# Hash-bucketed attention and a feed-forward layer in one kernel: work issued by an explicit list, weights cast while loading, uniform fallback added on VectorE, scores in two tiles

## The chip, the core and the metric

One core of a Trainium2 chip runs the kernel. It has five engines with in-order instruction queues of their own: TensorE (PE, matmul, with PEld for its weight loads), VectorE (DVE), ScalarE (ACT), GpSimd (POOL) and SyncE (SP, which here only issues DMAs). They meet at semaphores. The metric is device time in microseconds (us) of one launch.

## The reference, cut to what matters

Attention with a bucket mask: a query sees only keys whose six hash bits are the same as its own. Where no key matches, all scores are equal, and the softmax is uniform: the output is then the mean of all values. The result goes through a layer norm and a two-layer feed-forward block with a residual.

```python
q_bits = (einsum('bhsd,dk->bhsk', q, proj) > 0)       # k likewise
mask   = q_bucket[:, :, :, None] == k_bucket[:, :, None, :]
scores = where(mask, scale * q @ k.T, -1e9)
attn   = softmax(scores);  x = (attn @ v) as (B, S, 512)
xn     = (x - mean) / sqrt(var + 1e-6) * g_ln
out    = x + relu(xn @ w_ch1) @ w_ch2
```

B = 4 batches, 8 heads, 768 positions, 64 per head, w_ch1 512x2048, w_ch2 2048x512, all float32 outside.

## The kernel before, in words

A **unit** u (0 to 11) is 256 queries of one batch, three units to a batch. A **step** s (0 to 71, six to a unit) is one unit's 256 queries against 256 of the 768 keys, for one group g of four heads.

Per step: `scores` (L169) makes 24 matmuls into `sc`, a PSUM tile of four banks. Six bits of the hash `G` are multiplied first, and the two halves of q and k (`qb`, `kb`) are added in the same bank, so that a mismatch in the hash lowers the exponent by much. The four heads lie on four strips of 32 rows of the PE array. `exps` (L187) is one ACT instruction over the whole of `sc` to `E`. `av` (L201) makes 16 matmuls of `E` with the values `vaug` (64 columns and a one, which gives the row sum) into `acc`, two banks. At every third step `fall` (L191) first writes a tiny multiple of the sum of all values into `acc` with two matmuls: that is the uniform fallback. After three steps `normalize` (L213) divides on DVE and takes statistics; after six, `center` (L225) subtracts the mean into `xc`, and `flip` (L235) transposes `xc` into `xnT` by DMA.

Per unit then: `ff1` (L241), eight pieces of eight matmuls of 256 columns into one bank, each with a relu into `hb` on DVE (L252); `ff2` (L254), two times four quarters of four matmuls of 512 columns, each half ended by the residual sum `res` on DVE (L265), which `store` (L270) writes out. PSUM is full: four banks `sc`, two `acc`, one each for the tags `f1` and `f2`. So the next `scores` waits for `exps` of the last one, and an `ff1` in bank f1 for the relu of the one ahead.

Batch 0 is brought in by small pieces (`first`, L304): a 256-column piece of q or k is loaded, transposed on DVE in 32x32 blocks (L288), cast, hashed by four matmuls in float32 (`hf`, L301), and turned to bits (L86). Later batches go by whole groups (`load_x`, `turn_piece`, `cast_full`, `hash_mm`), and their bits are moved into `G` by 16 little DMAs a group (`hash_move`, L133).

Weights: `load_w1` (L311) loads w1 as float32 in four DMAs by SP into two buffers; `cast_w1` (L315) multiplies by g and casts, 16 DVE instructions. `load_w2` (L320) lets POOL issue DMAs that cast on the way.

The order of all this is a key per call: `at(key, fn, ...)` puts a call on a list, the list is sorted, and each engine runs its own instructions in that order. Steps have the key s, and the feed-forward pieces of the unit before are spread between them at 8.5 + 0.375 per piece.

Of the kernel before, what the change touches and what calls it, by code (L numbers as in the profile page):

```python
# [12 lines left out]


@with_exitstack
def kernel(
# [15 lines left out]
    nc = tc.nc  # L32
# [12 lines left out]
    EPS_ROW = 2.0 ** -100  # L45

# [3 lines left out]
    def qk_view(t, b, g):  # L50
        return t[b, 4 * g : 4 * g + 4].rearrange("i (tt r) d -> (i tt) (r d)", tt=TT)

    v_view = [v[b].rearrange("h (tt c kj) d -> c tt h (kj d)", tt=TT, c=CC) for b in range(B)]
    out_view = [out[b].rearrange("(tt c u qt) d -> u c tt (qt d)", tt=TT, c=CC, u=3) for b in range(B)]
    w1ap = moe_w_ch1.rearrange("(o p) h -> p o h", p=P)
    w2ap = moe_w_ch2.rearrange("(o p) d -> p o d", p=P)

    pfull = pool.tile([P, 2, P], F32, name="pfull")
    p32 = pool.tile([P, 2, 32], F32, name="p32")
    bias_sb = pool.tile([P, 1], F32, name="bias_sb")  # L60
    mhalf = pool.tile([P, 2], F32, name="mhalf")
    epsm = pool.tile([P, P], BF16, name="epsm")
    warm = pool.tile([P, 512], BF16, name="warm")
    g_sb = pool.tile([P, NDT], F32, name="g_sb")
# [3 lines left out]
    events = []  # L68

    def at(key, fn, *a):  # L70
        events.append((key, len(events), fn, a))

    qb, kb, G, vaug, vsum = {}, {}, {}, {}, {}
    X, T, vnat = {}, {}, {}
    sc, E, acc = {}, {}, {}
    xt, stats, rstd, xc, xnT, hb, f2, res = {}, {}, {}, {}, {}, {}, {}, {}
# [11 lines left out]
    def new_group(b, g):  # L88
        qb[b, g] = pool.tile([P, 2, S], BF16, name=f"qb{b}{g}", tag="qb", bufs=4)
        kb[b, g] = pool.tile([P, 2, S], BF16, name=f"kb{b}{g}", tag="kb", bufs=4)  # L90
        G[b, g] = pool.tile([P, 2, S], BF16, name=f"G{b}{g}", tag="G", bufs=4)

    def cast_q(eng, b, g, src, lo, hi):
        if eng is nc.scalar:
            nc.scalar.activation(qb[b, g][:, :, lo:hi], src, AF.Copy, scale=QS)
        else:
            eng.tensor_scalar(qb[b, g][:, :, lo:hi], src, QS, None, op0=AOP.mult)  # L97

    def load_x(b, g, t):
        X[b, g, t] = pool.tile([P, KJ * CC * D], F32, name=f"X{b}{g}{t}", tag="X", bufs=3)  # L100
        nc.sync.dma_start(out=X[b, g, t], in_=qk_view((q, k)[t], b, g))

    def turn_piece(b, g, t, n):
        if n == 0:
# [386 lines left out]
```

## Time and profile before

| | |
|---|---|
| median of 3 runs (lowest, highest) | 366.58 us (366.09, 366.65) |
| span of the profiled execution | 363.9 us |
| between span and median | 2.7 us |
| mean granted TensorE clock | 0.948 |
| busy: ACT, POOL | 144.7 us (40%), 100.5 us (28%) |
| matmuls, weight loads | 4281, 4344 (of the records in the trace) |

The span runs from the first to the last instruction. Busy times of engines overlap, and a PE shown busy need not be at its peak: matmuls are pipelined, so what a group of them costs is read from the distance between the start of one group and the start of the next.

### The profile page before, as it was taken

How to read it: one execution, taken by the hardware profiler on the slowest of the kernel's cores; microseconds unless marked ns; L12 is line 12 of the kernel's file. 1: busy time of each engine (PE TensorE's matmuls, PEld its weight loads, DVE VectorE, ACT ScalarE, POOL GpSimd, SP SyncE). 2: the span in 40 equal slices, each digit the busy share in tenths (PEclk: the TensorE clock that was granted, in tenths of full speed). 3: DMA queues.
4: the chain of work that ended last, by engine and by line, in shares of the span. 5: the costliest groups of instructions: out<-in, count | busy, mean ns of one | idle time of the engine just before them, and what ended most of it. 6: DMA issues, size and time to landing. Idle time of an engine off the chain costs nothing.

```text
span 363.9 us, 9678 instructions
## 1 busy us (share of the span) xinstructions
PE 312.7 (86%) x4281; PEld 209.8 (58%) x4344; DVE 183.3 (50%) x373; ACT 144.7 (40%) x76; POOL 100.5 (28%) x106
## 2 busy tenths in 40 slices
PE   8674457989988989989989989898889899897993
PEld 3353335766665666756656657666656567565561
DVE  1427245385662363578444534955624545446341
ACT  2344204662453554445246445533535455442000
POOL 1656142019940010069710010399200100101000
PEclk9989555899999999999999999999999999999899
DMA  7799931991021039860030279700210302203022
GB/s 170 174 243 212 306 112 29 273 260 23 9 64 34 3 88 278 193 141 7 12 78 13 59 204 242 192 7 8 64 35 2 88 2 59 31 2 78 10 59 58
DMA packets 34873, 35.68 MB, mean 98 GB/s; under 512 B 17424, under 2 KB 29712, under 8 KB 34832
## 3 DMA queue, kind: packets, MB, share of 16 engines
q1 hardware_dynamic: 31872, 32.96, 36.0%
q0 software_dynamic: 2112, 2.10, 3.6%
q8 instruction: 34, 0.56, 0.6%
q10 hardware_dynamic: 848, 0.01, 0.2%
q14 instruction: 7, 0.06, 0.1%
HBM read 27.27 MB, written 6.29 MB: 92 GB/s over the span
## 4 chain that ended last, share of the span: by engine, by line
PE 66%; DVE 15%; SPq 5%; DMA 4%; issue 3%; ACT 3%; POOL 1%; ACTq 0%; DVEq 0%; POOLq 0%
PE f L248 19%; PE f L258 18%; PE sc L182 11%; PE acc L206 8%; PE hf L301 4%; SPq L133 4%; DVE hb L252 3%; ACT E L189 3%; PE hp L123 2%; DVE xc L231 2%; DMA w1f<-in_moe_w_ch_dram 2%; DMA xnT<-xc 2%; PE warm L354 2%; DVE x L221 2%; DVE st L223 1%
## 5 line engine op out<-in xcount | busy, mean ns | idle before, releaser
L189 ACT ACTIVATE E<-sc,bias_sb 128x2048 bf16<-128x2048 f32 x72 | 141.6, 1967 | 173.9 <-PE sc L182 173.9
L248 PE MATMUL f<-xnT,w_sb 128*128 128x256 bf16 x768 | 99.7, 274 | 16.3 <-DVE hb L252 13.8
L248 PEld LDWEIGHTS <-w_sb 128*128 128x128 bf16 x768 | 72.4, 98 | 39.1 <-issue 23.0
L252 DVE TENSOR_SCALAR hb<-f 128x512 bf16<-128x512 f32 x96 | 65.6, 683 | 52.7 <-PE f L248 51.4
L258 PE MATMUL f<-w_sb,hb 128*128 128x512 bf16 x321 | 86.9, 385 | 3.5
L232 POOL TENSOR_SCALAR rs<-mv 128x2 f32<-128x2 f32 x12 | 6.1, 512 | 199.6 <-DVE mv L230 199.6
L182 PE MATMUL sc<-qb,kb 32*128 32x256 bf16 x1152 | 54.2, 275 | 0.0
L258 PEld LDWEIGHTS <-hb 128*128 128x128 bf16 x384 | 35.2, 99 | 30.5 <-issue 3.2
L206 PEld LDWEIGHTS <-E 128*128 128x128 bf16 x1152 | 43.1, 100 | 11.4 <-issue 10.5
L206 PE MATMUL acc<-vaug,E 128*128 128x65 bf16 x1152 | 49.5, 198 | 0.0
L265 DVE SCALAR_TENSOR_TENSOR res<-f,rs,x 128x512 f32<-128x512 f32 x24 | 18.0, 751 | 54.7 <-PE f L258 50.7
L182 PE MATMUL sc<-G 6*128 6x256 bf16 x576 | 41.9, 280 | 4.0 <-ACT E L189 3.9
L97 POOL TENSOR_SCALAR qb<-T 128x1536 bf16<-128x1536 f32 (+1 forms) x10 | 30.6, 3059 | 13.4 <-DVE T L288 13.4
L182 PEld LDWEIGHTS <-G 6*128 6x128 bf16 x576 | 15.4, 92 | 29.7 <-issue 28.6
L182 PEld LDWEIGHTS <-kb 32*128 32x128 bf16 x1152 | 30.8, 96 | 2.0
L301 PE MATMUL hf<-T,pfull 128*128 128x256 f32 x48 | 18.1, 514 | 13.6 <-DVE T L288 13.5
L83 DVE STREAM_TRANSPOSE T<-X 128x384 f32<-128x384 f32 x48 | 25.4, 555 | 0.0
L301 PEld LDWEIGHTS hf<-T,pfull 128*128 128x128 f32 x48 | 10.7, 246 | 18.7 <-DVE T L288 17.2
L223 DVE BATCH_NORM_STATS2 st<-x 128x6 f32<-128x256 f32 x48 | 18.1, 418 | 0.8
L221 DVE TENSOR_TENSOR x<-acc,rc 128x512 f32<-128x512 f32 x24 | 16.6, 692 | 0.8
L86 DVE TENSOR_SCALAR G<-hf 128x256 bf16<-128x256 f32 x12 | 5.1, 425 | 23.5 <-PE hf L301 23.5
L219 DVE RECIPROCAL rc<-acc 128x8 f32<-128x8 f32 x24 | 4.9, 205 | 21.1 <-PE acc L206 21.1
(35 smaller groups left out, 147.9 us busy)
## 6 DMA issues: line engine op xcount, KB each, us to landing
vnat<-in_v_dram SPq DMA_DIRECT2D x32, 192.0 KB
out_dram<-res SPq DMA_DIRECT2D x48, 128.0 KB
X<-in_q_dram SPq DMA_DIRECT2D x6, 768.0 KB
X<-in_k_dram SPq DMA_DIRECT2D x6, 768.0 KB
w1f<-in_moe_w_ch_dram SPq DMA_DIRECT2D x4, 1024.0 KB
w_sb<-in_moe_w_ch_dram POOLq DMA_DIRECT2D x4, 512.0 KB, 8.5
X<-in_q_dram SPq DMA_DIRECT2D x6, 256.0 KB
X<-in_k_dram SPq DMA_DIRECT2D x6, 256.0 KB
```

The costliest lines, as they stand in the source:

```text
L83: nc.vector.transpose(d[:, j, kj0 : kj0 + n], s[:, j, kj0 : kj0 + n])
L97: eng.tensor_scalar(qb[b, g][:, :, lo:hi], src, QS, None, op0=AOP.mult)
L182: nc.tensor.matmul(sc[s][:, i, 256 * kk : 256 * kk + 256], lh, rh, start=(rep == 0), stop=(rep == 2), skip_group_check=True,)
L189: nc.scalar.activation(E[s], sc[s], AF.Exp, scale=EXP_SCALE, bias=bias_sb)
L206: nc.tensor.matmul(acc[u, g][:, qt, (D + 1) * i : (D + 1) * (i + 1)], E[s][:, i, 256 * kk + P * qt : 256 * kk + P * qt + P], vaug[u // 3][ ...
L221: nc.vector.tensor_tensor(xo, a[:, :, :, 0:D], rc.to_broadcast([P, 2, 4, D]), op=AOP.mult)
L223: nc.vector.bn_stats(stats[u][:, qt, g], xt[u][:, qt, 256 * g : 256 * g + 256])
L248: nc.tensor.matmul(f1[:, n].rearrange("p (t x) -> p t x", t=2), w1_sb[:, dt, P * nt : P * nt + P], xnT[u][:, :, dt], start=(dt == 0), stop ...
L252: nc.vector.tensor_scalar_max(hb[u][:, 2 * p : 2 * p + 2], f1, 0.0)
L258: nc.tensor.matmul(f2[u, t], hb[u][:, nt, P * t : P * t + P], w2_sb[:, nt], start=(nt == 0), stop=(nt == NNT - 1),)
L265: nc.vector.scalar_tensor_tensor(res[u][:, t], f2[u, t], rstd[u][:, t : t + 1], xt[u][:, t], op0=AOP.mult, op1=AOP.add,)
L301: nc.tensor.matmul(hp[:, :256], pfull[:, j], tp[:, j], start=(j == 0), stop=(j == 1))
```

## The change

The kernel is the same in its arithmetic, apart from where the fallback, g and the casts are done. It has six parts.

- **Order.** The keys are replaced by a list of 1138 words, `ORDER`, each with an operation, the engine that runs it, and its indices: `S.t.14.2` is the scores of step 14 for all heads on TensorE, `R.a.2.4` the relu of unit 2, piece 4, on ACT. Each engine runs its words in the order of the list. Steps are taken out of order within a batch (14, 13, 12, 16), and ff1 pieces of a unit too.
- **Scores.** `sc` becomes two tiles of two banks (two heads each), and `exps` two ACT instructions of half the size, 144 for 72. In steps 0 to 9 the scores and the value matmuls of the two halves are also apart.
- **Fallback.** The 48 matmuls of `fall` go. The sum of the values over all keys is made once for each group of heads and batch by one matmul with ones (`sp`, 8 in all) and copied to `vsB` (`sc`), and a DVE instruction of 520 elements (`na`, 24 in all) adds it to `acc` into an SBUF tile `y`, on which the division works.
- **Weights.** w1 is loaded like w2, by four DMAs of POOL that cast. The 16 casts on DVE go, and g is applied in `ce`, where the centring becomes a DVE instruction with a second tensor (`gB`). The two xnT tiles of unit 0 are transposed by PE (`ft`) and copied (`fc`).
- **Relu.** 43 of the 96 run on ACT, 53 on DVE.
- **Start and end.** 32 warm-up matmuls of 128 columns for 24 of 512; one DMA of proj and copies for four DMAs; stores of the last unit in halves.

```diff
-        sc[s] = psum.tile([P, 4, 512], F32, name=f"sc{s}", tag="sc")
+        return ps(f"sc{s}{h}", [P, 2, 512], ("scA", "scB")[h])
-        nc.scalar.activation(E[s], sc[s], AF.Exp, scale=EXP_SCALE, bias=bias_sb)
+        nc.scalar.activation(E(s)[:, heads(h)], sc(s, h), AF.Exp, scale=EXP_SCALE, bias=bias_sb)
-        for qt in range(2):
-            nc.tensor.matmul(
-                acc[u, g][:, qt, : 4 * (D + 1)], epsm,
-                vsum[u // 3][:, 4 * g : 4 * g + 4].rearrange("p h e -> p (h e)"),
-                start=True, stop=False, skip_group_check=True,
-            )
+        vs = vsB(u // 3)[:, 4 * g : 4 * g + 4].rearrange("p h e -> p (h e)").unsqueeze(1).to_broadcast([P, 2, A])
+        nc.vector.scalar_tensor_tensor(
+            yt(u, g), vs, EPS_ROW, made[f"acc{u}{g}"][:, :, :A], op0=AOP.mult, op1=AOP.add,
+        )
-            nc.vector.tensor_scalar(xc[u][:, qt], xt[u][:, qt], mv[:, qt, 0:1], None, op0=AOP.subtract)
+        nc.vector.scalar_tensor_tensor(
+            xc(u)[:, t], xt(u)[:, t], mv(u)[:, t, 0:1], gB, op0=AOP.subtract, op1=AOP.mult,
+        )
-        nc.sync.dma_start(out=w1f[n], in_=w1ap[:, :, 512 * n : 512 * n + 512])
+        nc.gpsimd.dma_start(out=w1_sb[:, :, 512 * n : 512 * n + 512], in_=w1ap[:, :, 512 * n : 512 * n + 512])
-        nc.vector.tensor_scalar(
-            w1_sb[:, dt, 512 * n : 512 * n + 512], w1f[n][:, dt], g_sb[:, dt : dt + 1], None, op0=AOP.mult,
-        )
+        if eng is nc.scalar:
+            nc.scalar.activation(hb(u)[:, 2 * p : 2 * p + 2], f1, AF.Relu)
+        else:
+            eng.tensor_scalar_max(hb(u)[:, 2 * p : 2 * p + 2], f1, 0.0)
-        for _, _, fn, a in sorted(events, key=lambda e: (e[0], e[1])):
-            fn(*a)
+        for word in ORDER.split():
+            name, eng, *args = word.split(".")
+            OPS[name](ENGINES[eng], *map(int, args))
```

What this moves, at three places. First DVE ahead of the first feed-forward piece. In the kernel before, the casts of w1 (`w_sb`) stand between the last pieces of batch 0 (T and G), each with a weight DMA to wait for:

```order
L316 TENSOR_SCALAR w_sb<-w1f_172,g_sb 128x512 x4
L288 STREAM_TRANSPOSE T_449<-X_201 128x256 x2
L86 TENSOR_SCALAR G_104<-hf_453 128x256
L316 TENSOR_SCALAR w_sb<-w1f_205,g_sb 128x512 x4
L316 TENSOR_SCALAR w_sb<-w1f_460,g_sb 128x512
L288 STREAM_TRANSPOSE T_509<-X_203 128x256 x2
L86 TENSOR_SCALAR G_107<-hf_513 128x256
```

On the same engine of the changed kernel, the statistics and centring of unit 0 (st, mv, xc) stand there, with four transposes of batch 1 (`T_733`, which waits for the DMA of `X_731`) ahead of them:

```order
L442 TENSOR_TENSOR x_424<-y_578,rc_580 128x2x256 [waits DVE_49]
L244 STREAM_TRANSPOSE T_733<-X_731 128x384 [waits DMAHW0_49]
L244 STREAM_TRANSPOSE T_733<-X_731 128x384 x3
L446 BN_STATS st_533<-x_424 128x6 [waits DVE_49]
L446 BN_STATS st_533<-x_424 128x6
L449 BN_AGGR mv_740<-st_533 128x2 [waits DVE_49]
L450 SCALAR_TENSOR_TENSOR xc_742<-x_424,mv_740,gB 128x512 [waits DMAHW2_49,DVE_49]
```

The casts are gone from DVE; a load of the next batch is now ahead of unit 0's centring. Second, POOL in the same part of the program. Before, the four casting DMAs of w2 lie between its casts of kb and sums of values:

```order
L321 DMA w_sb<-in_moe_w_ch_dram 128x4x512
L295 CAST kb_106<-T_274 128x2x256
L321 DMA w_sb<-in_moe_w_ch_dram 128x4x512
L295 CAST kb_106<-T_326 128x2x256
L151 CAST vaug_92<-vnat_91 128x24x64
L321 DMA w_sb<-in_moe_w_ch_dram 128x4x512
```

After it, one DMA of w1 (L315), then the values of group 1 with the waits for their loads, then the three others and w2 (L318):

```order
L315 DMA w_sb<-in_moe_w_ch_dram 128x4x512
L328 CAST vaug_159<-vn_250 128x12x64 [waits DMAHW5_49,DMAHW6_49,DMAHW1_49,DMAHW0_49]
L328 CAST vaug_159<-vn_250 128x12x64
L336 TENSOR_TENSOR t_571<-vn_250 128x768 [waits Pool_49]
L338 TENSOR_TENSOR vsum_325<-t_571 128x256 [waits Pool_49]
L315 DMA w_sb<-in_moe_w_ch_dram 128x4x512 x3
L318 DMA w_sb<-in_moe_w_ch_dram 128x4x512 x3
```

So eight weight DMAs for four stand on POOL, three quarters of w1 behind the last values of batch 0. Third, ACT in the middle of the program. Before, it runs exponentials alone:

```order
L189 ACTIVATE E_2482<-sc_2457,bias_sb 128x2048
L189 ACTIVATE E_2564<-sc_2539,bias_sb 128x2048
L189 ACTIVATE E_2649<-sc_2614,bias_sb 128x2048
L189 ACTIVATE E_2731<-sc_2706,bias_sb 128x2048
L189 ACTIVATE E_2818<-sc_2793,bias_sb 128x2048
```

After it, pairs of halves, with a relu (hb) or a copy of the value sums (vsB) between some:

```order
L411 ACTIVATE E_2426<-sc_2400,bias_sb 128x1024
L411 ACTIVATE E_2426<-sc_2403,bias_sb 128x1024
L485 ACTIVATE hb_2170<-f_37_2434 128x512
L411 ACTIVATE E_2478<-sc_2455,bias_sb 128x1024
L411 ACTIVATE E_2478<-sc_2452,bias_sb 128x1024
...
L411 ACTIVATE E_2723<-sc_2700,bias_sb 128x1024
L351 COPY vsB_1677<-vp_2746 128x4x64
```

A relu on ACT so comes behind a pair of exponentials that may still run, and the next pair behind the relu.

More of the change, by code (lines that the diff above doesn't have):

```diff
@@ L66, with sb @@
     w2_sb = pool.tile([P, NNT, DM], BF16, name="w2_sb")
[L68 to L76, printed above, removed]
+    made = {}
+    def sb(name, shape, dt, tag, bufs):
+        if name not in made:
+            made[name] = pool.tile(shape, dt, name=name, tag=tag, bufs=bufs)
+        return made[name]
@@ L93, in cast_q, with cast @@
[L93 removed]
+    def cast(eng, t, dst, src):
         if eng is nc.scalar:
[L95 to L107 removed]
@@ L235, in flip @@
[L235 to L244 removed]
+            nc.vector.bn_stats(stats(u)[:, qt, g], xt(u)[:, qt, 256 * g : 256 * g + 256])
```

580 lines of the change are left out of this document (309 added, 271 removed).

## Prediction

> **What bounds the kernel now.** I read the page's busy times first, then the busy time by stage, then the timeline of PE in the two stages that differ, and last what PE waited for.
>
> ```profile
> span 363.9 us, 9678 instructions
> PE 312.7 (86%) x4281; PEld 209.8 (58%) x4344; DVE 183.3 (50%) x373; ACT 144.7 (40%) x76; POOL 100.5 (28%) x106
> ```
>
> PE is the only engine near its span. The median of the runs, 366.58 us, is 2.7 us above this span; I make the sum against the span and add 2.7 at the end. Busy by stage (start and end, length, busy time of PE, PEld, DVE, ACT and POOL, then the granted clock, the DMA share, GB/s):
>
> ```profile
> 0.00:10.00 10.00, 7.97 (x28) 3.47 (x28) 1.81 (x6) 1.91 (x2) 1.27 (x11) 1.00 0.82 174
> 10.00:20.00 10.00, 5.98 (x73) 4.13 (x74) 4.14 (x12) 5.07 (x4) 7.19 (x9) 0.95 0.79 174
> 20.00:30.00 10.00, 7.25 (x102) 5.02 (x99) 3.88 (x11) 3.80 (x2) 4.01 (x5) 0.88 1.13 248
> 30.00:40.00 10.00, 6.19 (x74) 3.96 (x74) 7.26 (x15) 2.10 (x2) 6.20 (x6) 0.80 1.08 227
> 40.00:50.00 10.00, 3.15 (x24) 2.08 (x20) 2.93 (x8) 1.97 (x1) 1.49 (x1) 0.50 0.87 282
> 50.00:65.00 15.00, 11.70 (x130) 7.99 (x131) 7.24 (x20) 4.62 (x3) 4.59 (x4) 0.50 0.13 26
> 65.00:337.00 272.00, 249.23 (x3745) 171.20 (x3804) 147.54 (x294) 125.21 (x64) 75.73 (x70) 1.00 0.35 85
> 337.00:341.00 4.00, 4.00 (x17) 1.77 (x15) 0.48 (x1) 0.00 (x0) 0.00 (x0) 0.65 0.01 2
> 358.40:363.90 5.50, 0.00 (x0) 0.00 (x0) 0.73 (x1) 0.00 (x0) 0.00 (x0) 0.98 0.36 95
> ```
>
> There are two kernels here. Up to 65 us PE is thinly used, at a falling clock; from 65 to 358.4 it is busy; then come 5.5 us of residual sum and stores. The timeline shows why the front is long:
>
> ```profile
> 39.06 1.67 DVE L316 TENSOR_SCALAR w_sb<-w1f,g_sb 128x512 bf16<-128x512 f32 x4
> 45.96 0.48 DVE L316 TENSOR_SCALAR w_sb<-w1f,g_sb 128x512 bf16<-128x512 f32 x1 [5.23 <-DMA w1f<-in_moe_w_ch_dram]
> 46.85 2.08 PE L301 MATMUL hf<-T,pfull 128*128 128x256 f32 x4 [5.78 <-DVE T L288]
> 65.00 1.89 PE L248 MATMUL f<-xnT,w_sb 128*128 128x256 bf16 x8
> ```
>
> DVE, in order, stands before a cast for 5.23 us until a w1 DMA lands; the transpose behind it is late, PE idles 5.78 us, the clock drops, and the first piece of ff1 starts at 65.0. By the order of the program 9 steps of scores and 8 of values are done there.
>
> In the dense stage I take the cost of a piece from start to start of groups:
>
> ```profile
> 206.21 0.66 PE L206 MATMUL acc<-vaug,E 128*128 128x65 bf16 x16
> 206.71 1.04 PE L248 MATMUL f<-xnT,w_sb 128*128 128x256 bf16 x8
> 207.58 1.03 PE L258 MATMUL f<-w_sb,hb 128*128 128x512 bf16 x3
> 211.42 0.39 PE L195 MATMUL acc<-vsum,epsm 128*128 128x260 bf16 x2
> 211.65 0.65 PE L206 MATMUL acc<-vaug,E 128*128 128x65 bf16 x16
> 213.96 0.29 PE L182 MATMUL sc<-G 6*128 6x256 bf16 x4
> 214.73 0.66 PE L206 MATMUL acc<-vaug,E 128*128 128x65 bf16 x16
> 352.14 6.21 PE L258 MATMUL f<-w_sb,hb 128*128 128x512 bf16 x27
> 84.83 1.51 PE L123 MATMUL hp<-T,p 128*32 128x192 f32 x32
> ```
>
> Values 0.50 us (206.21 to 206.71), ff1 0.87, fallback pair 0.23, scores 0.77; a quarter of ff2 0.86 (6.21 less some 0.17 of tail, by seven: the program has 28 there, one record is missing); a hash of a group 1.5. From 65.0 the kernel before still has 63 x 0.77 + 64 x 0.50 + 96 x 0.87 + 96 x 0.86 + 21 x 0.23 + 6 x 1.5 = 48.5 + 32 + 83.5 + 82.6 + 4.8 + 9 = 260.4 us of PE work, and takes 293.4. The 33.0 us between are 22.8 of idle (272.0 - 249.2), 1.4 of low clock (4.0 x 0.35), and 8.8 of seams between groups. PE's waits in that stage:
>
> ```profile
> PE f L248 <- DVE hb L252: 13.8, 11, 2.1
> PE hp L123 <- DVE hb L252: 2.4, 3, 0.8
> PE f L248 <- DMA xnT<-xc: 2.3, 2, 1.3
> ```
>
> (In all, how often, the longest.) Mostly ff1 waits for a relu that DVE reaches late.
>
> **The change, part by part.**
>
> *The front.* What must be done before the first ff1 (F.0.5) changes. By the list PE then has 10 hash pieces, 20 half scores, one full, 9 steps of values and the warm-up behind it. A hash piece is 1.04 us at full clock (the 2.08 above is at 0.50). A half of the scores lies between 0.39 (half the work) and 0.77 (two heads share the array where four did, and as many columns stream); I take 0.7, nearer to the full row, since columns set the pace. Sum: 10.4 + 14 + 0.8 + 4.5 and some 3.4 of warm-up = 33 us; from 1.7 us on, 35. ACT needs the exponentials of ten steps:
>
> ```profile
> L189 ACT ACTIVATE E<-sc,bias_sb 128x2048 bf16<-128x2048 f32 x72 | 141.6, 1967 | 173.9 <-PE sc L182 173.9
> L95 ACT ACTIVATE qb<-T 128x512 bf16<-128x512 f32 x2 | 1.2, 624 | 0.0
> L252 DVE TENSOR_SCALAR hb<-f 128x512 bf16<-128x512 f32 x96 | 65.6, 683 | 52.7 <-PE f L248 51.4
> L265 DVE SCALAR_TENSOR_TENSOR res<-f,rs,x 128x512 f32<-128x512 f32 x24 | 18.0, 751 | 54.7 <-PE f L258 50.7 <-DMA X<-in_q_dram 4.0
> L231 DVE TENSOR_SCALAR xc<-x,mv 128x512 bf16<-128x512 f32 x24 | 11.7, 487 | 1.0
> ```
>
> A half (1024 elements) lies between 0.98 us (half of 1967) and 1.25 (two of 624); on the line through 512 and 2048 elements it is 1.07, which I take. 20 x 1.07 = 21.4 us, from about 10 us (an estimate: two of the hash pieces and a transpose come first): 32. The DMAs: on DVE, four transposes of batch 1 stand ahead of unit 0's centring, so F.0.5 waits for X of batch 1.
>
> ```profile
> vnat<-in_v_dram SPq DMA_DIRECT2D x32, 192.0 KB
> w_sb<-in_moe_w_ch_dram POOLq DMA_DIRECT2D x4, 512.0 KB, 8.5
> ```
>
> SP issues 12 pieces of X of 256 KB (128 x 512 floats), 10 loads of values of 192, gB of 256 and that X of 768, 6016 KB; POOL beside it one to three weight DMAs, counted at 512 KB as in the row, or at 1024, as they read float32. By the GB/s of the stages 5960 KB have passed at 30 us and 8230 at 40: 6528 KB at 33, 9088 at 43. Behind this come the transposes, statistics, centring, PE transposes and copies, some 5 us (ten DVE or ACT pieces like those quoted): 38 to 48. PE's own 35 is the lowest end. I take **43**, the middle of the DMAs', since the other engines sum to less. The casts that go (16) are worth this shift, no term of their own.
>
> *What is left for PE at 43 us.* 61 x 0.77 + 63 x 0.50 + 83.5 + 82.6 + 9 + two hash pieces 2.1 + six `sp` matmuls 0.7 = 256.4 us. The fallback's removal is in it (4.8 from 260.4, and 0.7 back).
>
> *The stalls.* The loop scores, exponential, scores is tightest:
>
> ```profile
> 66.89 0.80 PE sc L182 x24
> 67.78 1.98 ACT E L189
> 69.79 0.84 PE sc L182 x24
> ```
>
> 2.90 us from start to start with nothing else between; with two halves (2 x 1.07 for 1.97) 3.07. By the list, PE work between the full scores of two steps sums to 3.0 to 6.1 us; eight places are under 3.07, by 0.56 once (18 to 20) and 0.06 elsewhere: 1.0 us. A relu on ACT (512 elements, 0.62) adds to the loop where it stands behind the pair with under 3.7 us of PE work: at most 20 places of half a microsecond, 10 us. Against it, the 13.8 and 2.4 us of waits for DVE go where relus are on ACT, for there DVE is in `na`, `nb`, `ce`. Idle then is 1 to 20 us; I take 7, as the work between two ff1 pieces mostly exceeds their relu too. With the seams, 8.8, that is **16**. If the cover is gone, the 33.0 of before stay.
>
> *DVE and the rest.* `na` adds 24 x 0.75 (as L265), `ce` 24 x (0.75 - 0.49); 43 relus leave (29 us), the casts leave. DVE ends near 50% again, beside PE, and I cost it at nothing. That cover breaks only if one chain of DVE comes late for the next ff1. The DMA transposes stay on SP between the same small moves: 0 to 2.3 us, in the 7. Start and end: the stores of the last unit in halves, 0 to -1 us of 5.5; I keep 5.5.
>
> A row on two engines of one memory:
>
> ```profile
> 31.72 1.81 POOL L164 TENSOR_TENSOR t<-vnat 128x768 f32<-128x768 f32 x1
> 32.31 3.89 DVE L316 TENSOR_SCALAR w_sb<-w1f,g_sb 128x512 bf16<-128x512 f32 x4
> ```
>
> The four casts took 3.89 us beside POOL's sums and 1.67 without (39.06, above). The Trainium skill, "SBUF — State Buffer", section "Who interferes with whom", says that a DVE instruction with two SBUF inputs, or in a two-port mode, and a GpSimd instruction that reads SBUF exclude each other; the trace agrees as far as the two-port kind goes. The rule speaks against the change: `nb` and `ce` now read two SBUF tensors, 48 instructions that did not. By it, each would stand behind POOL in 28% of cases (POOL's share), for about 1 us: 13 us of DVE, an estimate, and by the row's excess at most 2.2 us a time, 30 us. Either is in DVE's slack, so the sum stays by both.
>
> **Sum.** 43 + 256.4 + 16 + 5.5 = 320.9 us of span, with 2.7 around it **323.6 us**.
>
> **The rivals.**
>
> *A slow front: the clock stays at half.* Before, the clock was 0.50 from 40 to 65 us although PE was busy 11.70 of 15. If the new front has one gap like that of 5.78 us, its 33 us of work take up to twice as long: F.0.5 at 60, the time 60 + 256.4 + 16 + 8.2 = 340.6. For it: many in-order waits on two dozen DMAs. Against it: no weight stands ahead of batch 0's transposes now, and at 7.25 of 10 busy the clock was 0.88. The Trainium skill, "TensorE: Matmul & The Clock Gate", section "What's actually happening", says that an idle window of about 3.4 us halves the clock and a busy one restores it. The drop agrees; the return does not, in the 15 us quoted. By the rule the price would be smaller, one window. Chance 0.14.
>
> *The dense stage does not tighten.* The places may be chosen with other durations than the chip's; then other waits take the place of the 13.8, and 33.0 stay: 43 + 256.4 + 33.0 + 5.5 + 2.7 = 340.6. For it: the exponential's loop has 0.7 us of slack on average (3.8 of work against 3.07). Against it: that slack is everywhere positive or nearly so. Chance 0.14.
>
> *Slower: relus queue behind exponentials.* ACT is in order. If each of the 43 relus there waits for a whole pair (2.14 us), then runs 0.62, and PE has but one ff2 quarter (0.86) to cover it, PE loses 1.9 us each: 323.6 + 82 = 405. It passes 366.6 from 1.0 us each on. Against it: the list puts two to four groups behind most such relus. Chance 0.06.
>
> *It does not do what it says.* The first ff1 stays at 65 because the eight casting DMAs come late, and the stalls stay: 65 + 256.4 + 33.0 + 8.2 = 362.6. For it: three quarters of w1 are issued behind the last values of batch 0. Chance 0.04.
>
> **How the numbers follow.** The forecast has 0.62; with F.0.5 from 36 to 48 and 2 to 20 of idle its own range is 312 to 341. The first two rivals end inside 342, so the range is 310 to 342 and leaves out the last two and a little below, under 0.2. Faster by over 0.2% (about what a measurement here can tell from no change): 0.62 + 0.14 + 0.14 + most of 0.04 = 0.93; same 0.01; slower 0.06.
>
> **What would show it.** First ff1 in the timeline at 36 to 48 us, and the clock near 1.00 in 20 to 40. No L195 group; half exponentials of 0.98 to 1.25 us. From the first ff1 to the last matmul 272 us; PE idle there about 7, with no wait for a relu of over 1 us on average. Wrong it would be if `f` waits for ACT, if a POOL weight DMA is what ff1 or ff2 waits for, or if the front's clock is 0.50.

## The result, and the profile after

| | before | after |
|---|---|---|
| median (lowest, highest) | 366.63 us (366.09, 368.04), 5 runs | 321.83 us (319.59, 326.67), 5 runs |
| ratio, 95% interval | 1 | 0.8766 [0.8730, 0.8802] |
| span of the profiled execution | 363.9 us | 325.0 us (its time 326.67 us) |
| first ff1 matmul (F.0.5) | 65.0 us | 51.65 us |
| from there to the last matmul | 293.4 us | 268.3 us |

The profiled execution is the longest of the five, with a granted clock (the share of its full speed that TensorE is given) of 0.957 where the other four (319.59 to 322.12 us) had 0.980 to 0.983, so its front is longer than that of a usual run; ratios, here and below, leave out runs over 1.5% above the fastest of their kernel. The head of the page of after, and its row of the granted clock in 40 slices:

```profile
span 325.0 us, 9793 instructions
PE 310.7 (96%) x4320; PEld 211.8 (65%) x4320; DVE 182.9 (56%) x356; ACT 182.0 (56%) x198; POOL 91.5 (28%) x102
PEclk9995558999999999999999999999999999999999
```

PE is shown busy nearly as long as before (310.7 us for 312.7) in a span 39 us shorter. Busy time by stage, cut at the drop of the clock, at F.0.5 and behind the last matmul (start and end, length, busy time of PE, PEld, DVE, ACT and POOL, then the granted clock, the DMA share, GB/s):

```profile
0.00:24.00 24.00, 17.47 (x200) 13.21 (x201) 11.66 (x36) 11.02 (x11) 7.81 (x20) 1.00 0.99 211
24.00:51.65 27.65, 27.38 (x293) 18.23 (x291) 16.65 (x37) 13.74 (x13) 13.92 (x18) 0.51 1.05 202
51.65:320.00 268.35, 265.81 (x3834) 180.40 (x3830) 153.79 (x283) 157.20 (x174) 69.74 (x64) 1.00 0.33 84
320.00:325.00 5.00, 0.00 (x0) 0.00 (x0) 0.75 (x1) 0.00 (x0) 0.00 (x0) 0.96 0.22 52
```

The dense stage (third row) has 268.35 - 265.81 = 2.5 us of idle for 22.8 before. The front is now 24 us at the full clock, in which PE is busy for 17.47, and 27 us at half of it, in which PE is busy without a break. The run of the median has a span of 320.1 us; if its dense stage and end are as long as here, its first ff1 is at 320.1 - 268.3 - 5.0 = 46.8 us (an estimate). Of the 44.8 us between the medians the dense stage then gives 25.0 and the front 18. What PE waited for in the whole span (in all, how often, the longest):

```profile
PE hf L306 <- DVE tp L244: 4.2, 4, 2.4
PE vp L343 <- POOL vsum L338: 1.4, 2, 0.8
PE f L477 <- DVE hb L487: 0.5, 1, 0.5
PE sc L405 <- ACT E L411: 0.2, 1, 0.2
```

The waits for a relu (13.8 and 2.4 us before) have come down to 0.5, that for `xnT` (2.3) is gone, and no wait on an exponential of more than 0.2 us came in. The groups of the page that answer to those shown of before (busy, mean ns of one, idle time ahead and what ended it):

```profile
L411 ACT ACTIVATE E<-sc,bias_sb 128x1024 bf16<-128x1024 f32 x144 | 153.7, 1111 | 82.2 <-PE sc L405 80.3
L487 DVE TENSOR_SCALAR hb<-f 128x512 bf16<-128x512 f32 x53 | 36.6, 691 | 63.8 <-PE f L477 63.5
L485 ACT ACTIVATE hb<-f 128x512 bf16<-128x512 f32 x43 | 25.6, 596 | 20.6 <-PE f L477 20.5
L433 DVE SCALAR_TENSOR_TENSOR y<-vsB,acc 128x520 f32<-128x520 f32 x24 | 16.5, 689 | 9.0 <-PE acc L420 8.7
L450 DVE SCALAR_TENSOR_TENSOR xc<-x,mv,gB 128x512 bf16<-128x512 f32 x24 | 19.9, 829 | 0.9
```

ACT and DVE wait for PE (80.3, 63.5, 20.5 us), not PE for them. Last, three chains of the front. PE (some of its rows; start, length, and in brackets the idle time and what ended it):

```profile
23.18 1.13 PE L306 MATMUL hf<-tp,pfull 128*128 128x256 f32 x4 [2.42 <-DVE tp L244]
38.45 0.40 PE L343 MATMUL vp<-vsum,ones 128*128 128x256 bf16 x1
47.96 1.50 PE L420 MATMUL acc<-vaug,E 128*128 128x65 bf16 x24
49.27 1.04 PE L464 MATMUL ft<-ident,xc 128*128 128x128 bf16 x8
51.65 2.86 PE L477 MATMUL f<-xnT,w_sb 128*128 128x256 bf16 x24
```

DVE in the same stretch:

```profile
38.89 0.42 DVE L353 COPY vsB<-vp 128x256 f32<-128x256 f32 x1 [4.48 <-PE vp L343]
40.93 1.95 DVE L244 STREAM_TRANSPOSE T<-X 128x384 f32<-128x384 f32 x4
44.69 0.75 DVE L450 SCALAR_TENSOR_TENSOR xc<-x,mv,gB 128x512 bf16<-128x512 f32 x1
```

And POOL:

```profile
29.16 1.79 POOL L328 CAST vaug<-vn 128x768 bf16<-128x768 f32 x2 [3.31 <-DMA vn<-in_v_dram]
34.09 0.73 POOL L338 TENSOR_TENSOR vsum<-t 128x256 bf16<-128x256 f32 x1
```

POOL waits for the last load of the values and has their sums at 34.8. `vp` needs the sums, but stands in PE's queue behind scores and values at half clock, and runs at 38.45. DVE sat idle 4.48 us for it; the four transposes behind it, which need X of batch 1, waited for nothing. The centring is done at 45.4; PE takes the transposes of `xc` at 49.27, busy until then.

### The profile page after: what moved, and what is told of

Its sections match the earlier page's. It is cut to its first block, busy times and chain, and to the rows that moved or that the text cites. A ratio compares the mean times of both kernels' runs of the same rounds, so it can differ in the third digit from the quotient of the medians.

```text
span 325.0 us, 9793 instructions
## 1 busy us (share of the span) xinstructions
PE 310.7 (96%) x4320; PEld 211.8 (65%) x4320; DVE 182.9 (56%) x356; ACT 182.0 (56%) x198; POOL 91.5 (28%) x102
## 4 chain that ended last, share of the span: by engine, by line
PE 78%; DMA 8%; DVE 6%; SPq 4%; POOL 2%; issue 1%; ACT 0%; DVEq 0%; ACTq 0%
PE f L477 24%; PE f L492 23%; PE sc L405 17%; PE acc L420 11%; DMA X<-in_q_dram 4%; DMA vn<-in_v_dram 3%; SPq L382 2%; PE hp L370 2%; DVE xc L450 2%; DMA X<-in_k_dram 2%; PE hf L306 2%; SPq L292 1%; DVE st L446 1%; DVE x L442 1%; DVE y L433 1%
## 5 line engine op out<-in xcount | busy, mean ns | idle before, releaser
L411 ACT ACTIVATE E<-sc,bias_sb 128x1024 bf16<-128x1024 f32 x144 | 153.7, 1111 | 82.2 <-PE sc L405 80.3
L487 DVE TENSOR_SCALAR hb<-f 128x512 bf16<-128x512 f32 x53 | 36.6, 691 | 63.8 <-PE f L477 63.5
L405 PE MATMUL sc<-qb,kb 32*128 32x256 bf16 x1152 | 62.9, 281 | 0.0
L405 PEld LDWEIGHTS <-kb 32*128 32x128 bf16 x1152 | 35.5, 98 | 3.2
L485 ACT ACTIVATE hb<-f 128x512 bf16<-128x512 f32 x43 | 25.6, 596 | 20.6 <-PE f L477 20.5
L336 POOL TENSOR_TENSOR t<-vn 128x768 f32<-128x768 f32 x8 | 15.2, 1905 | 34.6 <-DMA vn<-in_v_dram 20.2
L328 POOL CAST vaug<-vn 128x768 bf16<-128x768 f32 x16 | 13.9, 889 | 39.0 <-DMA vn<-in_v_dram 30.3
L433 DVE SCALAR_TENSOR_TENSOR y<-vsB,acc 128x520 f32<-128x520 f32 x24 | 16.5, 689 | 9.0 <-PE acc L420 8.7
L450 DVE SCALAR_TENSOR_TENSOR xc<-x,mv,gB 128x512 bf16<-128x512 f32 x24 | 19.9, 829 | 0.9
L306 PE MATMUL hf<-tp,pfull 128*128 128x256 f32 x48 | 15.1, 447 | 5.2 <-DVE tp L244 4.2
L442 DVE TENSOR_TENSOR x<-y,rc 128x512 f32<-128x512 f32 x24 | 18.4, 767 | 0.8
```

The costliest lines, as they stand in the source:

```text
L306: nc.tensor.matmul(hf(g, t, kp)[:, :256], pfull[:, j], tp(g, t, kp)[:, j], start=(j == 0), stop=(j == 1))
L405: nc.tensor.matmul(sc(s, i // 2)[:, i % 2, 256 * kk : 256 * kk + 256], lh, rh, start=(rep == 0), stop=(rep == 2), skip_group_check=True,)
L411: nc.scalar.activation(E(s)[:, heads(h)], sc(s, h), AF.Exp, scale=EXP_SCALE, bias=bias_sb)
L433: nc.vector.scalar_tensor_tensor(yt(u, g), vs, EPS_ROW, made[f"acc{u}{g}"][:, :, :A], op0=AOP.mult, op1=AOP.add,)
L442: nc.vector.tensor_tensor(xo, a[:, :, :, 0:D], rc.to_broadcast([P, 2, 4, D]), op=AOP.mult)
L450: nc.vector.scalar_tensor_tensor(xc(u)[:, t], xt(u)[:, t], mv(u)[:, t, 0:1], gB, op0=AOP.subtract, op1=AOP.mult,)
```

## The experiments

"Dense" is the stretch from F.0.5 to the end of the last matmul in the profiled execution. A ratio is to the kernel before on the same chip.

**Is it the order of the list, or the parts?**

*e3: all relus on DVE, the list otherwise the same.*

```diff
-R.v.0.4 R.a.0.3 S.t.10.2 E.a.10.0 F.t.0.2 R.a.0.2 tu.v.1.0.1.2 CA.p.1.0.1 na.v.1.0 A.t.9.0 A.t.11.2 nb.v.1.0
+R.v.0.4 R.v.0.3 S.t.10.2 E.a.10.0 F.t.0.2 R.v.0.2 tu.v.1.0.1.2 CA.p.1.0.1 na.v.1.0 A.t.9.0 A.t.11.2 nb.v.1.0
...
```

> The changed kernel with all 96 relus on DVE (43 moved back from ACT), the list otherwise the same. Theory A (the split of the relus is what took away the 13.8 us of waits for DVE): DVE 183 + 43 x 0.69 - 0 = 213 us busy, PE waits for hb of 8 to 20 us come back, time 328 to 342. Rival (the order alone did it): waits for hb under 3 us, time within 3 us of 321.8.

Measured: 361.88 us (361.07 to 362.72), ratio 0.9893 [0.9841, 0.9945], more than any theory allowed. F.0.5 was at 48.74, so the front is not where it went; dense rose to 307.1 us. PE's waits:

```profile
PE f L477 <- DVE hb L487: 15.3, 10, 4.4
PE f L492 <- DVE res L497: 8.8, 5, 3.8
PE acc L420 <- DVE y L433: 5.0, 5, 1.8
PE hp L370 <- DVE hb L487: 3.0, 1, 3.0
```

DVE was busy 208 of 361 us, far from full, and yet the waits came back and spread to the residual sum and to `na`. (The last row is the hash of a later batch.) The relus do not add up to a full engine; 43 of them now stand in DVE's queue at places where `na`, `nb`, statistics and centring of a unit run, and each thing behind comes late. The waits cost more than their own time: in the dense stage the clock was at half in four stretches, 17.1 us in all, where after has none; that is 8.5 us of the 38.8 by which the stage is longer.

*e7: the kernel before, every other relu on ACT, in the old order.*

```diff
-        nc.vector.tensor_scalar_max(hb[u][:, 2 * p : 2 * p + 2], f1, 0.0)
+        if p % 2:
+            nc.scalar.activation(hb[u][:, 2 * p : 2 * p + 2], f1, AF.Relu)
+        else:
+            nc.vector.tensor_scalar_max(hb[u][:, 2 * p : 2 * p + 2], f1, 0.0)
```

> The kernel before with one part alone: the relus of odd ff1 pieces on ACT, 48 of 96, nothing else moved. Theory A (the waits for hb are DVE's load): of 13.8 us half or more go, time 355 to 361. Theory B (a place in the order is worth more than the engine: relus now stand behind exponentials of 1.97 us): waits of ff1 for ACT of 10 us or more come instead, time 364 to 380.

Measured: 365.81 us (364.77 to 367.48), ratio 1.0025 [1.0002, 1.0048]. One row of PE's waits says why nothing came of it:

```profile
PE f L248 <- DVE hb L255: 13.7, 11, 1.9
```

13.7 us for 13.8: taking half of the relus off DVE left the waits as they were. In the old order the late relus are those behind a unit's normalisation and centring, and that they share an engine with the other 48 did not matter: nine of the eleven waits are of 1.17 us in both kernels, each for the relu that stands behind the second `xc` of a unit. No ff1 waited for ACT either, so the waits bear out neither theory.

*e6: the kernel before, w1 by casting DMAs, and g in the centring, in the old order.*

```diff
-        nc.sync.dma_start(out=w1f[n], in_=w1ap[:, :, 512 * n : 512 * n + 512])
+        nc.gpsimd.dma_start(out=w1_sb[:, :, 512 * n : 512 * n + 512], in_=w1ap[:, :, 512 * n : 512 * n + 512])
-            nc.vector.tensor_scalar(xc[u][:, qt], xt[u][:, qt], mv[:, qt, 0:1], None, op0=AOP.subtract)
+            nc.vector.scalar_tensor_tensor(
+                xc[u][:, qt], xt[u][:, qt], mv[:, qt, 0:1], gB, op0=AOP.subtract, op1=AOP.mult,
+            )
```

> The kernel before with one part of the change alone: w1 by four casting DMAs of POOL at the same keys, no casts on DVE, g applied in the centring. Theory A (the weights' casts on DVE held the front): DVE's wait of 5.23 us and PE's idle of 5.78 us go, first ff1 at 50 to 58 us instead of 65.0, time 350 to 359. Theory B (the old keys hold the front whatever the casts do): first ff1 at 62 to 66, time 363 to 369.

Measured: 368.01 us (363.50 to 372.65, 10 runs), ratio 1.0017 [0.9970, 1.0064]. F.0.5 came at 61.34, 3.7 us earlier, and the dense stage gave it back:

```profile
PE f L250 <- DVE hb L254: 19.7, 11, 2.6
PE hf L303 <- DVE T L290: 9.9, 6, 4.3
```

The waits for a relu grew from 13.8 to 19.7: the centring, now 0.75 us instead of 0.49, stands ahead of it twice, and the nine waits of 1.17 us became 1.71. These 5.9 us are most of the 9.4 by which the dense stage is longer (302.8 us); the rest goes with the half clock, in three stretches of 3.41 us where before had one. The place of F.0.5 lies between the two theories; the time is as the second had it.

*e10: the kernel before with both of these and the fallback on DVE, in the old order, scores in one tile.* The edits of e6 and e7, and

```diff
+        vp = psum.tile([P, 512], F32, name=f"vp{b}{hs}", tag="f1")
+        nc.tensor.matmul(
+            vp[:, : 4 * (D + 1)], epsm, vsum[b][:, hs : hs + 4].rearrange("p h e -> p (h e)"), start=True, stop=True,
+        )
+        nc.vector.tensor_copy(vsB[b][:, hs : hs + 4].rearrange("p h e -> p (h e)"), vp[:, : 4 * (D + 1)])
-        for qt in range(2):
-            nc.tensor.matmul(
-                acc[u, g][:, qt, : 4 * (D + 1)], epsm,
...
+        nc.vector.scalar_tensor_tensor(
+            y, vs, EPS_ROW, acc[u, g][:, :, : 4 * (D + 1)], op0=AOP.mult, op1=AOP.add,
+        )
```

> The kernel before with three parts of the change together, in the old order and with the scores in one tile of four banks: the weights of the first feed-forward layer by casting DMAs with g in the centring, every other relu on ScalarE, and the uniform fallback by the sum of the values on VectorE. Theory A (the new order makes the gain; the parts only move load): 360 to 370 us. Theory B (the parts make it once they are together, since then no engine is in the way): under 345 us.

Measured: 399.04 us (397.12 to 400.02), ratio 1.0927 [1.0879, 1.0976]: worse than either theory. PE's waits:

```profile
PE f L257 <- DVE hb L264: 28.7, 13, 3.2
PE vp L171 <- POOL vsum L167: 18.8, 8, 6.1
PE hf L313 <- DVE T L300: 7.2, 6, 2.9
```

With `na` and the dearer centring on DVE the waits for a relu doubled, and PE stood 18.8 us before the eight sums. That second wait is owed to where I put the sum, behind POOL's addition of the values; in the list it costs 1.4 us. Both are matters of place. F.0.5 was at 60.2 us, so the loss is in the dense stage, 329.7 us: PE is idle there for 43.0 us (22.9 before), and its clock is at half in ten stretches of 3.41 us (one before). So these parts without the list cost 34 us, a good part of it by where the sums were put, the list without the relus on ACT loses 40 of its 45, and together they give all of it. The list with the other parts as before was not run, so how much the order gives alone stays open.

**Two score tiles.**

*e8: after, with one tile of four banks, and from step 10 on one exponential of 2048 elements.*

```diff
-        return ps(f"sc{s}{h}", [P, 2, 512], ("scA", "scB")[h])
+        return ps("scall", [P, 4, 512], "sc")[:, 2 * h : 2 * h + 2]
-        nc.scalar.activation(E(s)[:, heads(h)], sc(s, h), AF.Exp, scale=EXP_SCALE, bias=bias_sb)
+        if s < 10:
+            nc.scalar.activation(E(s)[:, heads(h)], sc(s, h), AF.Exp, scale=EXP_SCALE, bias=bias_sb)
...
+            nc.scalar.activation(E(s), ps("scall", [P, 4, 512], "sc"), AF.Exp, scale=EXP_SCALE, bias=bias_sb)
```

> The changed kernel with scores in one tile of four banks and one exponential of 2048 elements a step from step 10 on (62 of 72 steps; the list is the same, the exponential stands at the place of the second half). Theory A (halves buy nothing by themselves, they cost ACT 0.25 us a step): ACT 182 - 62 x 0.25 = 166 us busy, time within 2 us of 321.8. Theory B (the first half frees two banks early, and the values of a step or the next scores start sooner for it): PE waits for the exponential come up, time 325 to 335.

Measured: 340.40 us (340.17 to 341.18), ratio 0.9330 [0.9305, 0.9354]: outside both theories. Busy times of its front and of its dense stage but for the last 0.5 us, and PE's longest wait, all of it ahead of F.0.5:

```profile
28.00:65.00 37.00, 29.00 (x273) 19.00 (x275) 15.67 (x33) 14.17 (x14) 12.17 (x16) 0.50 0.86 155
65.70:334.00 268.30, 261.88 (x3789) 180.47 (x3830) 151.67 (x283) 147.52 (x112) 69.25 (x64) 1.00 0.31 81
PE scall L406 <- ACT E L413: 11.3, 11, 1.3
```

Dense is 268.8, for 268.3 in after. What is lost is in the front (F.0.5 at 65.7 us), where the halves of a step are apart in the list and the one tile makes each wait for the other's exponential; there the clock was at 0.50 for 37.5 us too. So the two tiles earn their keep in the first ten steps only.

**The fallback.**

*e4: 48 matmuls of zeros of the size of `fall` put back at their old place, ahead of the values.*

```diff
+        if first:
+            for qt in range(2):
+                nc.tensor.matmul(acc[:, qt, :A], ones, zz, start=True, stop=False, skip_group_check=True)
-                        start=(first and kk == 0 and i == range(4)[heads(h)][0]),
+                        start=False,
```

> The changed kernel with 48 matmuls of 260 columns put back on PE, two ahead of each group's values, here with zeros as the moving operand (the fallback stays on VectorE). Theory A (PE is the bound all through): 48 x 0.115 = 5.5 us more, time 326 to 329. Rival (the list has slack): within 2 us of 321.8.

Measured: 324.45 us (324.19 to 325.08), ratio 0.8877 [0.8840, 0.8914]. Dense was 272.8 us, 4.4 more than after's 268.3. By the medians it costs 2.6 us, by the ratios 0.011 of 366 us, which is 4.1; the runs of after spread over more than either, so I take the stage.

**The front.**

*e1: 40 matmuls of 128 rows and columns ahead of one hash piece of batch 1, into columns of its bank that nobody reads.*

```diff
+FILL = {(1, 0, 0): 40}
+        for _ in range(FILL.get((g, t, kp), 0)):
+            nc.tensor.matmul(hf(g, t, kp)[:, 256:384], ones, ones, start=True, stop=True)
```

> The changed kernel with 40 extra 128x128 matmuls of 128 columns put ahead of one hash piece (group 1, q, piece 0), into columns of its bank that nobody reads, where PE was idle 2.42 us and the granted clock then fell to 0.50 for 27.3 us. Theory A (that gap costs the clock, and the clock then costs time): granted clock at or near 1.00 until the first ff1, first ff1 at 40 to 45 us instead of 51.65, time 312 to 318. Theory B (the front is held by loads and by DVE and ACT, the clock only follows): first ff1 within 2 us of where it was, time within 1 us of 321.8, or later by the 2 us of extra matmuls.

Measured: 322.56 us (319.98 to 323.00), ratio 0.8808 [0.8758, 0.8858]. The gap of 2.42 us ahead of `hf` was filled and the clock did not fall at 24 us, but it fell at 37.5:

```profile
34.00:37.50 3.50, 2.81 (x56) 2.03 (x56) 3.00 (x7) 2.60 (x3) 3.50 (x6) 1.00 1.07 166
37.50:44.00 6.50, 6.50 (x78) 4.72 (x75) 4.76 (x11) 4.50 (x5) 3.28 (x5) 0.50 1.24 205
```

F.0.5 was at 45.05 in the profiled execution, of 319.98 us. The median is that of after: its usual runs, by their clock of 0.980 to 0.983, do not seem to have the early drop, and the added matmuls cost something.

*e2: 58 more of them, ahead of six other pieces.*

```diff
+FILL = {(0, 1, 2): 6, (1, 1, 0): 6, (1, 1, 1): 16, (1, 0, 0): 40, (0, 0, 1): 10, (1, 1, 2): 10, (1, 0, 1): 10}
```

> As the run with 40 extra matmuls, and besides them 6 to 16 ahead of six other hash pieces of the front (58 in all, 3.2 us at full clock). Theory A: the clock is at 1.00 in every run whatever the phase of its window, time 311 to 317, with less spread than 319.6 to 326.7. Theory B: 1 to 4 us later than the run with 40.

Measured: 322.54 us (321.89 to 324.36), ratio 0.8830 [0.8785, 0.8876]. F.0.5 at 47.4; the clock was at half from 38.5 to 48.7. No gain.

*e5: the last load of batch 0's values issued earlier by SP, and the four transposes of batch 1 moved behind the centring on DVE.* (`lv` is that load, `lg` the load of gB, `tu` the transposes, `ce` the centring.)

```diff
-ca.p.1.1.2 lg.s ...
+ca.p.1.1.2 lv.s.0.4.2 lg.s ...
-LX.s.1.0.0 tu.v.1.0.0.3 tu.v.1.0.0.0 tu.v.1.0.0.1 tu.v.1.0.0.2 nc.v.0.1 ce.v.0.1 ft.t.0.1 fc.a.0.1 ce.v.0.0 rs.p.0
+LX.s.1.0.0 nc.v.0.1 ce.v.0.1 ft.t.0.1 fc.a.0.1 ce.v.0.0 tu.v.1.0.0.3 tu.v.1.0.0.0 tu.v.1.0.0.1 tu.v.1.0.0.2 rs.p.0
```

> The changed kernel with two moves in its list: the last load of batch 0's values (lv.s.0.4.2) issued ahead of gB and the third pieces of q, and the four transposes of batch 1 (tu.v.1.0.0.*) behind unit 0's centring. Theory A (the first ff1 waits for the chain last values, POOL's sums, the fallback sum on PE, DVE's statistics and centring): the values' cast on POOL starts at 24 to 26 us instead of 28 to 29, first ff1 at 40 to 43 us in a run whose clock holds, time 315 to 320. Theory B (PE's own work at the granted clock sets the first ff1): first ff1 within 1 us of 45 to 51, time 319.6 to 323.

Measured: 321.03 us (318.56 to 325.84), ratio 0.8772 [0.8724, 0.8820], not to be told from after. The profiled execution (325.84) had F.0.5 at 51.45, with the clock at half from 28 to 52. It is no clean test of the transposes: with the earlier load, the `nb` at 25.19 us took 3.33 us on DVE beside POOL's addition of the values, PE stood 2.6 us for the `G` behind it, and the clock fell in that gap. e11, below, has the same with its rows.

*e9: e1, and a matmul of zeros over the whole array in each half-head of the scores of steps 5 to 9, to hold the clock.*

```diff
+                    if rep == 0 and 5 <= s < 10:
+                        nc.tensor.matmul(
+                            sc(s, i // 2)[:, i % 2, 256 * kk : 256 * kk + 256], ones, zz,
+                            start=False, stop=False, skip_group_check=True,
+                        )
```

> The kernel after, with the 40 full matmuls of 128 columns ahead of the hash pieces of batch 1 and, new, one matmul of zero weights by a 128 x 256 tile into the scores of each half-head of steps 5 to 9 (40 more; they add zero to the scores, some 40 x 0.107 = 4.3 us of PE work at the full clock). Theory A (the clock stays up only while the whole array is at work, and the front of the kernel is set by PE's own in-order work at the granted clock): the clock stays above 0.97 from 10 to 45 us, the first feed-forward matmul starts at 42 to 44.5 us, and the time is 316 to 320 us. Theory B (the chain of the values, their sums on GpSimd, the copy and the normalisation on VectorE sets the first feed-forward matmul near 45 us whatever the clock, or the added work eats what the clock gives): first feed-forward matmul at 45 to 48 us, time 321 to 324 us.

Measured: 342.84 us (340.64 to 344.67), ratio 0.9378 [0.9321, 0.9435]: both theories fall. Dense is 268.2, F.0.5 at 65.7. Its busy times, cut where the clock changes:

```profile
30.00:35.50 5.50, 5.50 (x40) 2.54 (x38) 2.38 (x7) 2.23 (x2) 5.34 (x8) 1.00 1.05 319
36.00:39.00 3.00, 3.00 (x39) 2.15 (x36) 0.00 (x0) 1.11 (x1) 3.00 (x5) 0.50 1.12 167
39.50:42.00 2.50, 2.50 (x27) 1.24 (x25) 0.87 (x2) 1.11 (x1) 0.00 (x0) 1.00 1.24 204
42.50:65.50 23.00, 23.00 (x167) 9.81 (x166) 6.85 (x15) 7.27 (x7) 2.30 (x3) 0.50 0.70 115
```

The clock fell between 35.5 and 36 us, behind 5.5 us in which PE was busy all the time, half of it on the whole array (a hash piece and eight matmuls of zeros, some 1.1 and 1.7 us). And the added matmuls cost far more than the 0.107 us each that I had counted, as its PE timeline shows:

```profile
31.29 0.28 PE L410 MATMUL sc<-G 6*128 6x256 bf16 x1
31.50 0.28 PE L415 MATMUL sc<-zz,ones 128*128 128x256 bf16 x1
31.72 0.28 PE L410 MATMUL sc<-G 6*128 6x256 bf16 x1
31.93 0.28 PE L415 MATMUL sc<-zz,ones 128*128 128x256 bf16 x1
32.14 0.39 PE L410 MATMUL sc<-qb,kb 32*128 32x256 bf16 x4
32.37 0.27 PE L410 MATMUL sc<-G 6*128 6x256 bf16 x1
```

Eight matmuls take 1.08 us here, from 31.29 to 32.37. Without the zeros (the next run, at the same clock) the six take 0.34, from 27.09 to 27.43: the matmuls of two heads, on two strips of rows, no longer overlap when one over all rows lies between. That is 0.37 us for each zero matmul, 15 us for 40 at the full clock, and more at half of it.

*e11: e1 and e5 together.* The diffs of both.

> The kernel after, with both changes to its front that had been tried apart: the 40 full matmuls ahead of the hash pieces of batch 1, and the last load of the values of batch 0 issued earlier with the four transposes of batch 1 behind the centring. Theory A (the front is set by the chain load of the values, casts and sums on GpSimd, copy and normalisation on VectorE, and the half clock behind it; with both out of the way the first feed-forward matmul moves): first feed-forward matmul at 41 to 43.5 us, last matmul 267 to 269 us behind it, median 316.5 to 319 us. Theory B (PE's own in-order work ahead of it sets 45 us whatever the chain does, and the added matmuls cost what the clock gives): first feed-forward matmul at 44.5 to 46 us and a median of 320 to 323 us, not to be told from the kernel after on the same chip.

Measured: 328.59 us over 6 runs (321.89 to 330.63), five of them 327 to 331. The best, 321.89, is still above the two best of e12 on the same chip (317.40, 319.59), so this is no gain, and both theories fall. F.0.5 at 51.9, dense 268.7. Its PE timeline shows what came ahead of the profiled run's half clock:

```profile
27.09 0.28 PE L405 MATMUL sc<-G 6*128 6x256 bf16 x2
27.43 0.27 PE L405 MATMUL sc<-G 6*128 6x256 bf16 x2
30.29 0.28 PE L405 MATMUL sc<-G 6*128 6x256 bf16 x2 [2.37 <-DVE G L245]
```

PE stood 2.37 us, and the clock fell at 31. On DVE stood `nb`:

```profile
26.80 3.10 DVE L442 TENSOR_TENSOR x<-y,rc 128x512 f32<-128x512 f32 x1
40.82 0.69 DVE L442 TENSOR_TENSOR x<-y,rc 128x512 f32<-128x512 f32 x1
```

3.10 us, for 0.69 the second time. The earlier load had moved POOL's work on the values onto it, a cast from 25.87 to 27.47 us and the addition:

```profile
27.54 1.80 POOL L336 TENSOR_TENSOR t<-vn 128x768 f32<-128x768 f32 x1
```

The Trainium skill, "SBUF — State Buffer", section "Who interferes with whom", says that a DVE instruction with two SBUF inputs contends with a GpSimd instruction that reads SBUF; `nb` has two, and these rows agree, with 2.4 us lost.

*e12: after, unchanged, on that chip.*

> The kernel after itself, unchanged, beside the other run on the same chip. Theory A (its spread of 319.6 to 326.7 us is the clock ahead of the first feed-forward matmul and nothing in the stage behind it): the profiled run lies between 318 and 327 us, its last matmul ends 267 to 269 us behind the first feed-forward matmul, and that first matmul is at 45 to 52 us, later by as much as the time is longer. Theory B (the spread comes from the dense stage, by transfers or the clock there): the stretch from the first feed-forward matmul to the last one differs from 268.3 us by 2 us or more.

Measured: 323.17 us (317.40 to 325.61, 6 runs), ratio 0.8708 [0.8651, 0.8765]. The profiled execution took 324.0 us with F.0.5 here:

```profile
49.02 2.86 PE L477 MATMUL f<-xnT,w_sb 128*128 128x256 bf16 x24
49.02:316.52 267.50, 265.56 (x3834) 1.00 0.35 88
```

(The second row: the stretch to the end of the last matmul, PE's busy time, clock, DMA share, GB/s.) Against after's profiled execution F.0.5 is 2.63 us earlier and the time 2.67 us shorter; dense is 267.5 for 268.3. The first theory holds for this pair: the difference is in the front. That it is so in every run was not measured, since the others have no profile; a part of the spread lies outside the span, which is 1.7 to 2.8 us shorter than the time in these six runs.

The profiled executions of all kernels with the list and the relus on ACT, side by side (the half clock is that which set in between 24 us and F.0.5, to its end, and in brackets the same in steps of 3.41 us):

| | at half clock, us | F.0.5, us | dense, us | time, us |
|---|---|---|---|---|
| e1 | 6.8 (2) | 45.05 | 268.2 | 319.98 |
| e4 | 10.2 (3) | 45.6 | 272.8 | 325.08 |
| e2 | 10.2 (3) | 47.4 | 269.0 | 323.07 |
| e12 (after) | 13.7 (4) | 49.0 | 267.5 | 324.0 |
| e5 | 23.9 (7) | 51.45 | 267.7 | 325.84 |
| after | 27.3 (8) | 51.65 | 268.3 | 326.67 |
| e11 | 20.5 (6) | 51.9 | 268.7 | 327.33 |
| e9 | 3.4 and 23.9 (1, 7) | 65.7 | 268.2 | 340.64 |
| e8 | 37.5 (11) | 65.7 | 268.8 | 341.18 |

Dense is the same within 1.5 us but for the work that e4 adds. What differs is the front. The lengths are whole multiples of 3.41 us, so in these traces the clock changed only in steps of that length. The step that ended with its return held, in all nine, most or all of the eight transposes `ft` of 128 rows and columns, which run up to 2.4 us ahead of ff1; the return itself came ahead of F.0.5 in five (44.30 for 45.05 us in e1) and behind it in four.

## Why the prediction came out

323.6 us was forecast and 321.83 measured, inside the range. In the terms of the sum the profiled execution reads 51.65 + 256.4 + 11.9 + 5.0 + 1.7 = 326.7, for 43 + 256.4 + 16 + 5.5 + 2.7. Two terms were off and set each other off: the front was put 4 us (by the 46.8 us estimated above) to 9 too short, the stalls 4 too long. That the total came within 2 us is luck to that extent. Of the prediction's own signs, two spoke against it in the profiled execution: its front was at 0.50, and F.0.5 lay outside 36 to 48 us. The others held: no ff1 waited for ACT, none for a weight DMA.

- **The front, 43 us: mis-sized, and for the wrong reason.** The step that failed is "on DVE, four transposes of batch 1 stand ahead of unit 0's centring, so F.0.5 waits for X of batch 1". The trace shows those transposes at 40.93 us without a wait. DVE had waited 4.48 us before them for `vp`, which stood behind PE's own work at half clock; after the centring `xc` waited again, 3.8 us, for PE. The prediction had summed PE's work ahead at 33 us at the full clock, 35 with its start, and called that the lowest end. The work was sized about right, 17.47 + 27.38 / 2 = 31.2 us by the rows of after; left out were 6.5 us of waits in the first 24 us and the 13.7 us that the half clock adds, and so PE's own work became the bound. 45 to 52 us was measured. e5 moved the transposes behind the centring, and nothing came of it, though its own new wait came in their place. What a front without any half clock would take was not reached in any run.
- **First rival, the slow front: it came true in part.** "One gap like that of 5.78 us" was to cost 17 us. A gap of 2.42 us was enough, and the price from e1 to after was 6.6 us, for 20.5 us more of half clock. The prediction also misread the trace of before, as in its own row of 30 to 40 us (0.80) the clock had already fallen ahead of that gap, which runs from 41.07 to 46.85. PE's row in the half microsecond of the fall (length, busy time, clock, DMA share, GB/s):

```profile
36.00:36.50 0.50, 0.20 (x6) 0.53 1.02 397
```

What came ahead of it was a gap of 2.60 us, to 35.31, of the size of that in after. The prediction set the drop and the return against the Trainium skill, "TensorE: Matmul & The Clock Gate", section "What's actually happening" (one idle window of about 3.4 us halves the clock, a busy one restores it). The drop came behind gaps shorter than that window; the length of 3.41 us agrees. Here too the return disagrees: 27.38 us busy of 27.65 at 0.51. That the window runs freely, so that the same kernel varies from run to run, which the section also says, agrees with after and e12.
- **What is left for PE, 256.4 us, with the seams of 8.8: right.** The two sum to 265.2 us, and the dense stage holds 265.8 us of busy PE. The trace gives only their sum.
- **The stalls, 16 us: 11.9.** Idle was 2.5 us for the 7 of the forecast. The step that was mis-sized is the relu on ACT between two pairs of exponentials ("at most 20 places of half a microsecond"): PE never waited for ACT there, 0.2 us in all. That the waits for DVE go was right; e3 and e7 show that neither the list with all relus on DVE nor relus on ACT in the old order removes them.
- **Half an exponential, 1.07 us: 1.111.** 144 x 0.04 = 6 us more of ACT, which waits for PE 80 us; nothing of it shows.
- **The fallback, 4.8 us saved: 4.4 in the dense stage (e4).** Right.
- **DVE, costed at nothing: right, in the list's order.** `na` was 0.689 (0.75 forecast), `ce` 0.829. With 43 relus more, and 208 of 361 us busy, it made PE wait (e3). The forecast's warning, that its cover "breaks only if one chain of DVE comes late for the next ff1", is what e6 and e10 show in the old order. Over the medians of `ce` and `nb`, 24 x (829 - 752) + 24 x (767 - 692) ns = 3.6 us in all were lost in after. That is the most that two inputs in SBUF beside POOL can have cost there, less than the 13 or 30 us by the rule or by the row; in e5 and e11 one such overlap came at a bad place.
- **Second rival, the dense stage does not tighten: no.** Third, relus behind exponentials: no; it needed 1.0 us for each of 43 to undo the gain, and PE waited 0.2 us for ACT in all. Fourth: no, F.0.5 did not stay at 65.

What stays open is what the clock counts: in every profiled run of the table it came back for good within 1.4 us of the first ff1, in a step with the transposes `ft`, and none tells why. Nor is the gain of the front split among the parts: e6 gives 3.7 us to the weights in the old order and e8 14 (profiled executions) to 19 (medians) to the two tiles in the list, and the list itself, the warm-up and the DMA of proj were not run alone. No run here was faster than after beyond the noise.

## What to carry to other kernels

Ask of a part that takes load off an engine what stands in that engine's queue ahead of the late instruction: half the relus off DVE changed nothing in the old order, and nearly as many back on DVE cost 40 us in the new one. Sum the work that PE must do in order ahead of a stage at both clocks, and take the larger with a chance of its own wherever PE is thinly used or waits for loads. A second score tile pays where the halves are computed apart; where they follow each other it changed nothing.

## What the runs showed of the hardware

- The granted clock can be at 0.50 with PE busy throughout: 6.50 of 6.50 us in e1, 23.00 of 23.00 in e9, 27.38 of 27.65 in after. In all of them the work was mostly scores on strips of 6 and 32 rows, values of 65 columns, a few hash pieces, and in e9 the zeros. It rose for good within 1.4 us of the first ff1 matmul, ahead of it in e1 (44.30 for 45.05 us) and e12 (48.16 for 49.02), where the eight transposes `ft` of 128 rows and columns had run; e9 had it up for 3.41 us before.
- The clock changed in steps: its stretches at half were 2, 3, 3, 4, 6, 7 and 8 times 3.41 us long (e1, e2, e4, e12, e11, e5, after).
- It can fall without an idle gap (e9, ahead of 36 us, behind 5.50 busy of 5.50). Gaps of 2.42, 2.37 and 2.60 us were followed by a fall in after, e11 and before.
- A matmul over all 128 rows between matmuls on strips of rows cost 0.37 us at the full clock, where it lasts 0.21 from start to start; the starts show that those around it no longer overlap (e9).
- A DVE instruction with two inputs in SBUF, 0.69 us alone, took 3.10 us (e11) and 3.33 us (e5) beside POOL's work on the values.
